# A filter regrouped inside SBUF, masks in spare rows, and a new order, in a two-part sequence layer

## The chip, the cores and the metric

One core of a Trainium2 chip. The metric is the device time of one execution in microseconds (us), median of several runs.

## The reference, cut to what matters

Two independent layers over 2048 tokens and 640 channels, their outputs side by side.

```
# A: a causal long convolution over tokens, per channel
k_shift = sum over t of k_pad[:, t:t+S] * shift_k[:, 3-t]      # short filter, 4 taps
kv = k_shift * v
y  = irfft(rfft(kv, 2S) * rfft(ssm_k, 2S))[:S] + kv * ssm_D    # long filter ssm_k: (640, 2048)
a  = q * y
# B: attention with a memory, 32 heads of 20, four segments of 512 tokens
for s in range(4):
    p     = softmax(q_s k_s^T * scale + causal mask)           # 512 x 512 per head, inside the segment
    a_dot = p @ v_s
    a_mem = phi(q_s) M / (phi(q_s) z + 1e-6)
    o     = g * a_mem + (1 - g) * a_dot
    M, z  = M + phi(k_s)^T v_s, z + sum phi(k_s)
b = concat(o) @ wo
out = concat([a, b], axis=-1)
```

## The kernel before

**Recorded, then issued by hand.** The kernel's functions do not issue instructions. They record steps (`Recorder.add`), each with an engine and a key such as `("A", 1, "FK", 0)`; `Recorder.issue` then issues all steps in the order of a list packed into the text `ORDER`, and puts each group of PSUM banks where the list `BASE` says. So every instruction of the trace carries the line of that one helper, L256, and groups are told apart by tiles. The list fixes, for each engine, the order of its instructions; SP issues nearly all DMAs, in its order.

**Part A, `conv(dp)`,** runs over five blocks of 128 channels, dp = 0 to 4. Steps of a block, by key:
- `sk`, `kt` or `sz`, `st` (`load_filter`): the long filter of the block, tokens on partitions, in tile kT, partition p holding tokens 8p to 8p+7 of either half of the sequence. Block 0 is turned by PE (`kt`). Blocks 1 to 4 go another way: a transposing DMA brings tokens 128m + p to partition p, one DMA (`sz`) writes that to a scratch in memory, the tile `turned`, and two DMAs (`st`) read it back in the wanted grouping. The ring kT has two buffers: one for the transposed load, one for the result.
- `lk`, `lc`, `lv`, `ks` (`short_filter`): k comes in transposed (kr), for blocks 2 to 4 with shifted copies (kb, kr); the 4 taps are matmuls with scaled unit matrices (skd), which ACT makes from the taps; the product with v lies in vt.
- `FK`, `FX` (`spectrum`): matmuls with the table Wf, copied out of PSUM into F by ACT or DVE as a fixed text of bits (`EVICT`) says; `BK`, `BX` are the sums behind them on DVE. `P1`, `P2`, `P3`, `YB` (`product`) are DVE work, `I` and `O` (`inverse`) matmuls with Wi, the product with q (`lq`), and the stores.

**Part B** runs over u = 0 to 7: segment u // 2, half of the heads u % 2. `project(u)`: `P` and `V` are the projections (five matmuls each); the results go to KQ, which holds per head 32 columns: 20 of k or q, one for the softmax bound, 11 zeros. `KT` is a transposing DMA from KQ to KQT, so that a head lies on 32 partitions, four heads on 128. `kam` and `bound` compute the bound, `rows` are four small DMAs that write it into row 20 of q in KQT. `attend(u)`: the steps `S` fill PSUM with scores, four heads side by side on row groups of 32: D are the four diagonal 128 x 128 blocks, A and J those below; ACT's exponential turns each into ET (160 instructions). `O` are the matmuls with Va, `N` the division, `W` the output projection, `OB` its stores.

The mask of a diagonal block is added in PSUM by matmuls ahead of the scores: four strips of 32 columns, for each head one matmul of mleft (128 columns) with mright broadcast over the four blocks.

```python
for i in range(4):
    for hl, bank, r, g in heads:
        nc.tensor.matmul(bank...[:, :, 32 * i:32 * i + 32], lhsT=self.mleft[r, 96 - 32 * i:224 - 32 * i],
                         rhs=self.mright[r, None, :].to_broadcast([32, 4, 32]), start=(i == 0), stop=False, ...)
```

Of the kernel before, what the change touches and what calls it, by code (L numbers as in the profile page):

```python
# [44 lines left out]
def small_consts():  # L45
    p = np.arange(128)
    d = p % 32
    hl = p // 32
# [4 lines left out]
    epsrow = np.zeros((128, 4), np.float32)
    for hh in range(4):
        rows = (hl == hh) & (d < DH)
        maskbd[rows, hh, 0:DH + 1] = 1.0
# [9 lines left out]
    return sel.astype(BF16_NP), maskbd.astype(BF16_NP), epsrow, mleft.astype(BF16_NP), mright.astype(BF16_NP)  # L66
# [198 lines left out]
class Layer:  # L265
    def __init__(self, ctx, tc, A_q, A_k, A_v, A_shift_k, A_ssm_k, A_ssm_D, B_x, B_wq, B_wk, B_wv, B_wo, B_beta, out):
# [18 lines left out]
        sel_np, maskbd_np, eps_np, ml_np, mr_np = small_consts()  # L285
# [36 lines left out]
        parts = [sel_np, ml_np, mr_np, np.concatenate([np.eye(64)] * 2).astype(BF16_NP), maskbd_np, eps_np.view(BF16_NP)]  # L322
# [5 lines left out]
        sel, ml, mr, id2, mb, eps = [pack[:, int(a):int(b)] for a, b in zip(at, at[1:])]  # L328
# [110 lines left out]
    def conv(self, dp):  # L439
# [8 lines left out]
        def load_filter():  # L448
            key("sk")
            sk = self.ring("kT", [128, 4, 4, 128], n=2)[:].rearrange("p a b d -> p (a b d)")  # L450
            kT = self.ring("kT", None)
            if dp in TURN:
                nc.sync.dma_start(out=sk, in_=self.ssm_k[dsl, :])
                skv = sk.rearrange("d (a p h c) -> d a h c p", a=2, h=2, c=4)
                for c in range(4):
                    key("kt", c)
                    g = self.group(1, "kt")
                    with rec.one():
                        for b in range(4):
# [65 lines left out]
        def spectrum(kind, src):  # L525
            F = self.ring("F", [128, 4, 2, 512], n=FBUF)
            for c in range(4):
                key("F" + kind, c)
                for i in range(2):
                    if i % FW == 0:  # L530
                        g = self.group(FW, "F")
                    with rec.one():
                        for j in range(2):
                            o = g.ap[:, i % FW, 256 * j:256 * j + 256]
                            last = kind == "K" and c == 0 and i == 0
                            for h in range(2):
                                rhs = src[:, h:4:2, c, :]
# [210 lines left out]
    def attend(self, u):  # L748
# [10 lines left out]
        def block(bank, hl, g, kc, q0, n, **kw):  # L759
            r = slice(32 * hl, 32 * hl + 32)  # L760
# [149 lines left out]
    def project_out(self, s):  # L910
# [41 lines left out]
        for t in range(4):  # L952
# [37 lines left out]
ORDER = r"""  # L990
c-jTQ17H{c3<SVW@|kUSwr$&9XWO=I+qOCz?QGk&&ATkfifqV^9LR}W$c;RR3P&UWrBE4VQ2}|857kf_RZs>Ikz6Z6kRRoc29Z%78Bi4kP!OR|2$c{8g^@xHd6cMwn#il^v<SLD5r|sIglLG4#E5}dh>w`as<Dwx
Q)+e8KsTh)L`aPcS{n(FUDKi-(rW`WLtXSmX0$>^?TW%$A4Rk|LL&*<ps2<}3p7Fr6hjV8hSn&iP0$@}kz0GBA&P51v_uK*jmGGKd|FbQB8#R&JM=<+O|5;<9vv_cX*G>@M1K^;P$WlZbV6JdM=4E+LRvrvql|{d
AdE(79fq7b5~&ad127gtFb2ah3S~8uPSbH1f$<oov$dQS)NPoqnYDrr*YY|=$7)J6(2UrQ%?O8FIssF)l1@Y%Ou|k~#tzKUaXJMJwIrrvu2$7XIu-MD7sl%doq=jvT_@-?jMR!6gc|x-D{C#?k186dqqL^Z#BS8l
#=2N%p^1*x+Ij%Zbua4b9xT#*SfWj}na<F9T3_d2rXIvew9rGCjiuT_Pa!GJVzQ3W`MMPywWTi5R(cL|p%zIxso64JsHYKvdFZM0aR#&__@%wIwJtyamTNC{JB|}*qbqbFW@$J5t<kK9F2YJ(itx4t6Lpn#*P~dB
wz>?HG>RO<CS9#jEV{MVc6t~~5Y-~sAKk2Lw2uzZff`wY(OK7Oc=Xl3dL3Q0i-xtExQ~81NC)e3oJW7XgcZ1esB#gPv0iT@oL#{XeTa>E73(yfZP3`Z8aEJ4hUzUmMjU&DHF$!R2xEKn0m4aiiEOJ7L*m*~tj8Vf
)n|xr`*ok*#X-G?1hxTd5mRDWB0Hel^f@}%Is};54n3>ewWGa29El}yWg}kVoNhv53)1ttRpUu)Nn)?CMf+JN+o}Dnv$eMHvRmUz1RT*_n$%t+x&2dEB6)+vlFSZi8+(VNdP<M!TLj2yO<`yBum)=q3DM))My}}z
eUFrOQa_-lwX_IwU2o`Rjc73}m0iOpw6fH4MI+fqT-D@qK|dp=rI3{J73q=CB1(7rf?jq}Q`;pCWohK5-qmkNW4H94hPK<9O43?pyRW^ihy6fSODcEtf&RmHJk%_fOnxD)^sxkzPO@1-d8FCxFMeWxrL#OX(0(I_
QPNvp>tY$Ko8_}Va7iy+Eu&?!p*GCgS_Ww$?JU1RhS(s>BzdKP6*Q5-*4Oe$A<HParLd`7vLa@Z(?Ure8E%<ngypg<QdHVWPAMz}CAa05kygywN@y8nDNx*sNf9YwxnzuWkdju^3dvZjX$7Q|WtZ<3XzeYll(v~R
&T3gTYcI3xrR9+E_Q8Hw4HH(kS611I%LEG}A5Hnwx=0l(Arq~KRJBqv$vVnp`(<UVla!RM(oK5G6dP@2th1D}3Rd1;+Y{|BrDdv>k+AZ{{#hmKBh##(RJ6VV&bD$g*ZRvRt8I1cv(>dZHr-}eDAu#r8k#MozCF_h
w$K{cb8T#8rJ=piCf3vzSu=Z~i_O`PVc6W}SvZE}5Sec+?5%#Ym%6~->0di4?YZ3ETX?o$BYv^+(t#1V!iGvq4v>|$#8z20S#1?$jXl+Y^3@`-lB~7gw#=5Aah<i2KUPs9aJ!MmC6LW{Ox9avsn5vVX*+DMHD^_6  # L1000
z$ok`QMupt*)WODjW$B6$tK%in{A|=kRXf3+T3DQq_=FfT{c{*%O3lxHRP=gk{EoiyX~DFwwSCf!PZ(rtS!H5U1`T7_Ct@_E3GBRY_J@+nml0Nv=$FqO^L;LJY;d$ij8@~x^s%mkU*&;+iaAaw9|IR&RQFuv(YkE
;_`!bVQY?&_-w+d(vjn2lGI^rcI9}PCm(gDbmC-5!1LCWb$QAb$b9L>CX$HL<g8q<gq$v?Bq@7vp`4eK(o}jfIWO8z?abahCv&8pB;zcZE3>5!FGv6zNn$491Ubz5l7fpQCHt}-8%RGkmc!Ce`tvPQ@f}lhAk*;$
(=a_>asbmZ1DD8R8N`gt!}lD_i?UQQF)#CRnLJ}=HkajcNt#I^e&BsRXJJ0%1LkKDKH>@~z#GiUUR)_dn2p()gSS|amn~R|G7EF^CWrI1tdiR-&RiVEGctn3Sb{_Og{4`BWjT_$xmwEczFd{^tiV#dD{JH_OY)OG
kZV$rW4Tt!_(b{2&w5YpSS40w6;|aqe&%?N;t_enb@GkXc*X8oS-)kkIEJJ7gZFq@Ub8xH%LbXi8m#5F?TTENpDgT?IFsw;i%w*q&tehZD6<(Nb2ynd<c@5Yn=+L}{TJtQ9&gDsPT?k*!H@jSivEe4Wjc3AG5^Es
wu+VfhCP(kEahvsO&-Zs`Od$b&jnn_MO@6%{*PN^E#X13j_X;&mvAY?E4%x0uHa5t$;WbsHT|uqKamZ5CQs!qzsoMUXH|S7H*vSTlV=vzpUYKyA@pV3BhT%nY~>FL=hrN}o9~rZQr}<8P20wOvYGY#jRbK!ckrWZ
VFTaE_fpb7$SyYWpYmBgNhtp+zhu8O_Ahck9y5%8liw1-cQdp<v?jiXb^QtdNJM{Rk$f-raX%w_RDWVo`~VN~sa5x;p3<B7KRLwIUcvuLIgjS4yoKMl=pNHwSS*k2aa<G{!yj0APv*(JxgV0ap2AytJa6S`JecYH
pj7n)p3oDyX&Vpl_@34i`)R5^wrZZ<&+sIVFo|dMOrF6{F@#5%#oKvS&*s@Zhf~k8hiCSr-r9S)>oMl^T;A4u`enBF;|#5N`~<Hsly>yIp3fV4ZtvioJiizBa}1*eyt8-l^9-k5J*-|}3Ge0wy|#zfI^Nr(X?MTK
e%{~v_$3bTfj-Im`c+2IK|a|F`CuR8Q+&0L^N2dshxu?H;n%pv$9q&A;$uCEuJkxM!K3R)ALXljhDX-KI?-qQb;i|MKF8<!XrJeiG>K02`99MZ_*!4*F*K%5^JE%NW9f8X=!-moF7_q9)R*~kkFD!{g>UdZ9$%B{
5kKk)b+2#qM7qfXbi42HoxaO=`#wMB`~A3|@PmHH4|}j5@DShZLB7Se`ZoU$7|Gh+
"""  # L1010
# [76 lines left out]
```

## Time and profile before

| | |
|---|---|
| median of 3 runs | 270.21 us (270.09 to 271.11) |
| profiled execution | 269.69 us, of which the span of the instructions 267.9 us |
| granted TensorE clock | 1.00 |
| PE, DVE, ACT busy | 258.5, 246.6, 249.2 us |
| DMA packets | 131516, 44.72 MB, of these 121899 under 512 bytes |
| memory read, written | 14.05 MB, 7.34 MB |

PE is TensorE's matmuls, PEld its weight loads, DVE VectorE, ACT ScalarE, POOL GpSimd, SP SyncE; SPq is SP's queue, which issues DMAs. A row of a timeline gives start and length in us, engine, operation, out<-in by the program's names, and a count; idle time before it stands in brackets with what ended it. A row of a group gives the count, then busy us and the mean ns of one, then idle time before it. A row of one tile's instructions gives shortest, median and longest duration in ns, then first and last start. A row of stretches gives the stretch, its length, busy us (and count) of PE, PEld, DVE, ACT and POOL, then the granted clock, the DMA engines' share, and GB/s. A row of waits: who waited for whom, us in total, how often, the longest.

### The profile page before, as it was taken

The numbers are of one execution on the slowest core, as the hardware profiler recorded it, in microseconds if no ns is written. First come the engines' busy times: TensorE is split into PE (matmuls) and PEld (weight loads), VectorE is DVE, ScalarE is ACT, GpSimd is POOL, SyncE is SP. The second block draws the span as 40 slices with busy tenths as digits, with TensorE's granted clock in tenths as the row PEclk, the third lists the DMA queues.
The fourth block names the chain that finished last, engine by engine and source line by source line (L and its number), as shares of the span: only waits on it lengthen the run. The fifth ranks groups of instructions, "written<-read, shape, count | busy, mean of one in ns | idle before, by whom it ended". The sixth has DMA issues, their size and how long they took to land.

```text
span 267.9 us, 10042 instructions
## 1 busy us (share of the span) xinstructions
PE 258.5 (96%) x4335; PEld 193.4 (72%) x4335; DVE 246.6 (92%) x387; ACT 249.2 (93%) x392; POOL 7.2 (3%) x18
## 2 busy tenths in 40 slices
PE   8999999999999999999999999999999999989994
PEld 3788678768777787878677777778776876666781
DVE  0399999999999999999999999999999999999971
ACT  2695899999999999999999999999999999999953
POOL 8200000000000000000000000000000000000000
PEclk9999999999999999999999999999999999999999
DMA  7999899988979979997997799998970194545124
GB/s 212 279 224 162 208 231 214 202 257 173 190 156 250 209 145 182 223 187 154 181 209 168 176 184 182 182 171 135 171 168 8 47 160 107 126 102 125 39 51 128
DMA packets 131516, 44.72 MB, mean 167 GB/s; under 512 B 121899, under 2 KB 129072, under 8 KB 131344
## 3 DMA queue, kind: packets, MB, share of 16 engines
q1 hardware_dynamic: 131328, 43.96, 81.3%
q8 instruction: 34, 0.56, 0.9%
q0 software_dynamic: 144, 0.12, 0.1%
q14 instruction: 10, 0.08, 0.1%
HBM read 14.05 MB, written 7.34 MB: 80 GB/s over the span
## 4 chain that ended last, share of the span: by engine, by line
PE 60%; ACT 27%; SPq 5%; issue 3%; DVE 3%; DMA 2%; ACTq 0%; DVEq 0%
PE ps L256 60%; ACT ET L256 18%; SPq L256 5%; ACT F L256 3%; DMA vt<-in_A_v_dram 2%; ACT KQ L256 2%; ACT PP L256 1%; DVE Kh L256 1%; ACT Va L256 1%; DVE vt L256 1%; ACT outb L256 1%; ACT qabs L256 0%; DVE F L256 0%; DVE kam L256 0%; ACT xT L256 0%
## 5 line engine op out<-in xcount | busy, mean ns | idle before, releaser
L256 ACT ACTIVATE ET<-ps 128x1024 bf16<-128x1024 f32 x160 | 160.4, 1092 | 0.2 <-PE ps L256 0.2
L256 PE MATMUL ps<-wqkv,xT 128*128 128x320 bf16 x480 | 77.6, 299 | 0.5 <-ACT xT L256 0.3
L256 PEld LDWEIGHTS <-xT 128*128 128x128 bf16 x640 | 57.1, 98 | 27.8 <-issue 6.8
L256 ACT CAST F<-ps 128x512 bf16<-128x512 f32 x72 | 42.4, 651 | 0.3 <-PE ps L256 0.3
L256 PE MATMUL ps<-Va,ET 128*128 128x21 bf16 x1280 | 42.0, 173 | 0.0
L256 PEld LDWEIGHTS <-ET 128*128 128x128 bf16 x1280 | 39.2, 96 | 2.3 <-issue 1.2
L256 PE MATMUL ps<-KQT 32*128 32x128 bf16 (+2 forms) x896 | 35.3, 239 | 1.0 <-DVE o L256 0.5
L256 PEld LDWEIGHTS <-Wf 128*128 128x128 bf16 x320 | 29.8, 98 | 6.3 <-issue 1.2
L256 ACT CAST KQ<-ps 128x320 bf16<-128x320 f32 x54 | 24.6, 497 | 3.3 <-PE ps L256 3.3
L256 PE MATMUL ps<-wo,xT 128*128 128x320 bf16 (+2 forms) x160 | 25.5, 299 | 1.3 <-ACT ET L256 1.3
L256 PEld LDWEIGHTS <-KQT 32*128 32x128 bf16 x896 | 16.7, 92 | 10.8 <-issue 9.3
L256 PE MATMUL ps<-kT,Wf 128*128 128x256 bf16 x160 | 22.0, 273 | 0.2 <-ACT ET L256 0.2
L256 PE MATMUL ps<-vt,Wf 128*128 128x256 bf16 x160 | 21.6, 272 | 0.0
L256 PE MATMUL ps<-Y,Wi 128*128 128x256 bf16 x160 | 20.8, 273 | 0.0
L256 DVE TENSOR_TENSOR o<-ps,rr 128x640 bf16<-128x640 f32 x24 | 19.6, 818 | 0.4
L256 DVE TENSOR_TENSOR Y<-Y,pq 128x2048 bf16<-128x2048 bf16 (+1 forms) x20 | 18.5, 936 | 0.0
L256 PE MATMUL ps<-Mbd,PqT 128*128 128x84 bf16 x96 | 18.3, 202 | 0.1
L256 DVE TENSOR_TENSOR pq<-Xh,Kh 128x2048 bf16<-128x2048 bf16 x15 | 18.2, 1212 | 0.0
L256 PEld LDWEIGHTS <-Wi 128*128 128x128 bf16 x160 | 14.8, 98 | 2.5 <-issue 0.6
L256 PE MATMUL ps<-skd,kr 128*128 128x128 bf16 (+4 forms) x116 | 16.6, 257 | 0.0
L256 PEld LDWEIGHTS <-kr 128*128 128x128 bf16 x116 | 14.6, 149 | 2.3 <-issue 1.1
L256 PE MATMUL ps<-pack 32*128 32x128 bf16 x512 | 14.8, 217 | 0.9 <-ACT ET L256 0.8
(86 smaller groups left out, 359.8 us busy)
## 6 DMA issues: line engine op xcount, KB each, us to landing
vt<-in_A_v_dram SPq DMA_DIRECT2D x10, 256.0 KB
pq<-in_A_q_dram SPq DMA_DIRECT2D x10, 256.0 KB
turned<-kT SPq DMA_DIRECT2D x4, 512.0 KB
kT<-turned SPq DMA_DIRECT2D x8, 256.0 KB
out_dram<-pq SPq DMA_DIRECT2D x8, 256.0 KB
out_dram<-outb SPq DMA_DIRECT2D x12, 160.0 KB
kb<-kr SPq DMA_DIRECT2D x6, 256.0 KB
Wf<-c_wf SPq DMA_DIRECT2D x4, 256.0 KB
```

The costliest lines, as they stand in the source:

```text
L256: f(*[fix(a) for a in args], **{k: fix(v) for k, v in kw.items()})
```

## The change

1. `load_filter`, blocks 1 to 4: the scratch in memory goes, with its write and its two reads. The transposed load is issued in two halves of 1024 tokens, interleaved in the buffer. Eight DMAs from SBUF to SBUF (`ss`, m = 0 to 7) then regroup it: each reads 128 partitions of 512 bytes and writes 16 partitions. kT's layout becomes (h, c, a, d), so that the filter's spectrum reads 256 elements in one run; block 0 copies out of PSUM into that layout.
2. The 11 spare columns of KQ are no longer zero. For the 11 token positions 116 to 126 of every 128, spare column r of k is 1 where the position is above 116 + r, and spare column r of q is -1e30 where the position equals it. So the scores matmul of a diagonal block masks those 11 query columns itself, and the fourth mask strip covers 20 columns instead of 32. Position 127 needs no mask. Score matmuls below the diagonal use 21 of the 32 rows.
3. In the set-up on POOL, the fill of 1536 elements of KQ is replaced by a small fill and two copies from the constants in `pack`.
4. ORDER and BASE are new: 1508 steps instead of 1482 (24 more on SP, 2 more on POOL). EVICT is the same text with zeros behind it that no copy reaches.

What the unpacked lists say of the order: on PE, the step `taps` moves from place 21 to place 10, straight behind the ten warm-up matmuls; the second projection P.0.3 from place 39 to 36, ahead of three of the four ks steps; three V.0 steps to places 41 to 43, ahead of all FX.0 steps; seven projections stand between the bound of u = 0 and the first S step in place of six. On ACT, four of the skd steps stand ahead of its third copy of xT in place of none. From place 60 to 490 of PE's 510 the lists differ by moves of at most six places, and at the end the W.3 steps are swapped. On SP, the eight ss of block 1 stand in the places 38 to 46, the last just ahead of the first q load of block 0.

```diff
+    spare = 31 - DH
+    own = np.arange(127 - spare, 127)
+    step = np.zeros((128, 2, spare), np.float32)
+    step[:, 0] = np.arange(128)[:, None] > own[None, :]
+    step[:, 1] = MASKED * (np.arange(128)[:, None] == own[None, :])
...
-        self.turned = [dram.tile([S, 128], bf16, name=f"turned{i}") for i in range(5)]
...
-        nc.gpsimd.memset(self.KQ[:, :, :, :, DH:32], 0.0)
+        nc.gpsimd.memset(self.KQ[:, :, 1, :, DH:DH + 1], 0.0)
         nc.gpsimd.memset(self.KQ[:, :, 0, :, DH:DH + 1], 1.0)
+        steps = step.rearrange("p (i r) -> p i r", i=2)
+        for i in range(2):
+            nc.gpsimd.tensor_copy(out=self.KQ[:, :, i, :, DH + 1:32], in_=steps[:, None, i, None, :].to_broadcast([128, 4, 16, 31 - DH]))
...
-            kT = self.ring("kT", None)
+            kT = self.ring("kT", None)[:].rearrange("p (h x) c d -> p (h x c d)", h=2).rearrange("p (h c a d) -> p h c a d", h=2, c=4, a=2)
...
-            z = self.turned[dp]
-            nc.sync.dma_start_transpose(out=sk.rearrange("p (m d) -> p m d", d=128), in_=self.ssm_k[dsl, :])
-            key("sz")
-            self.queue("sz", dp).dma_start(out=z[:].rearrange("(m p) d -> p m d", p=128), in_=sk.rearrange("p (m d) -> p m d", d=128))
-            key("st")
-            self.halves(self.queue("st", dp), kT, z, slice(0, 128))
+            sk = sk.rearrange("p (m a d) -> p m a d", m=8, a=2)
+            for a in range(2):
+                nc.sync.dma_start_transpose(out=sk[:, :, a, :], in_=self.ssm_k[dsl, 1024 * a:1024 * a + 1024])
+            for m in range(8):
+                key("ss", m)
+                nc.sync.dma_start(out=kT[16 * m:16 * m + 16].rearrange("p h c a d -> p (h c) (a d)"), in_=sk[:, m].rearrange("p a d -> p (a d)"))
             return kT
...
-                                rhs = src[:, h:4:2, c, :]
+                                rhs = src[:, h, c] if kind == "K" else src[:, h:4:2, c, :]
...
-        def block(bank, hl, g, kc, q0, n, **kw):
-            r = slice(32 * hl, 32 * hl + 32)
+        def block(bank, hl, g, kc, q0, n, rows=DH + 1, **kw):
+            r = slice(32 * hl, 32 * hl + rows)
...
                 for i in range(4):
+                    n = 32 if i < 3 else DH
                     for hl, bank, r, g in heads:
-                        nc.tensor.matmul(bank.rearrange("p (b q) -> p b q", b=4)[:, :, 32 * i:32 * i + 32], lhsT=self.mleft[r, 96 - 32 * i:224 - 32 * i],
-                                         rhs=self.mright[r, None, :].to_broadcast([32, 4, 32]), start=(i == 0), stop=False, grp=g, skip_group_check=True)
+                        nc.tensor.matmul(bank.rearrange("p (b q) -> p b q", b=4)[:, :, 32 * i:32 * i + n], lhsT=self.mleft[r, 96 - 32 * i:224 - 32 * i],
+                                         rhs=self.mright[r, None, 0:n].to_broadcast([32, 4, n]), start=(i == 0), stop=False, grp=g, skip_group_check=True)
...
-                        block(bank[:, 128 * kc:128 * kc + 128], hl, gg, kc, 128 * kc, 128, start=False, stop=(kc == 3), grp=g)
+                        block(bank[:, 128 * kc:128 * kc + 128], hl, gg, kc, 128 * kc, 128, 32, start=False, stop=(kc == 3), grp=g)
```

More of the change, by code (lines that the diff above doesn't have):

```diff
@@ L65, in small_consts @@
         mright[32 * h:32 * h + 32] = MASKED * (np.arange(32)[None, :] <= j[:, None])
-    return sel.astype(BF16_NP), maskbd.astype(BF16_NP), epsrow, mleft.astype(BF16_NP), mright.astype(BF16_NP)
+    spare = 31 - DH
[3 more added lines that the diff above has]
+    step[:, 1] = MASKED * (np.arange(128)[:, None] == own[None, :])
+    return sel.astype(BF16_NP), maskbd.astype(BF16_NP), epsrow, mleft.astype(BF16_NP), mright.astype(BF16_NP), step.astype(BF16_NP)
 QUEUES = {"sync": "SP", "scalar": "ACT", "vector": "DVE", "tensor": "PE", "gpsimd": "POOL"}
@@ L275, in __init__ @@
         rec = self.rec = Recorder(tc, psum.tile([128, 8, 512], f32, name="ps"))
-        dram = E(tc.tile_pool(name="dram", bufs=1, space=bass.MemoryType.DRAM))
-        self.turned = [dram.tile([S, 128], bf16, name=f"turned{i}") for i in range(5)]
-        rec.scratch = {t[:].tensor.name for t in self.turned}
         nc = self.nc = rec.nc
@@ L327, in __init__ @@
         nc.gpsimd.dma_start(out=pack[:], in_=self.real.inline_tensor(np.ascontiguousarray(np.concatenate(parts, axis=1)), name="c_pack").ap())
-        sel, ml, mr, id2, mb, eps = [pack[:, int(a):int(b)] for a, b in zip(at, at[1:])]
+        sel, ml, mr, id2, mb, eps, step = [pack[:, int(a):int(b)] for a, b in zip(at, at[1:])]
         self.sel, self.mleft, self.mright = sel, ml, mr
@@ L994 @@
[L994 to L997, printed above, removed]
@@ new lines @@
+t+o^smAX<(>Pr@hDM_T1RJ01#L<(CoDP?h_m86z#Qd}BIQ%Nh7tWwE(NN8ywb*#CxkjBzlN?ToPBSoy9)wg!iRsy7<w3n2UP8wKuNiQv>p(U06Qo~Y7BkL;}q^ER{;+9YbNMkD@{iL_lw8~b-I!OZQC4Ho*6|<_=
+Q98?D87>2*i6xh=(nU(jP#Gd)WxR}#(NfN8TNoK6!(^O{l&03q#z-w|Zeb;!OpsBs#n#zYn<xt`(DuoCTW&3_tSz(^w!x~{M%!j_WxJJ@7S_u$%YF$bljML*mR2@JrpjNNCNrd+wYJ_iQw~ZWn=V`BkgT*tHcNI{
+d+T7UY_WB;HrCmWN?S`NYps)Yu_ZQJw#Z@WW__)nEw!$8Oa|H<36>z+V<FPrcH0rzYyEA2ZL%KL(>B|2xhR8do`jbZGFL{~VB2Sx<f`nj(Kf`c$$UwGWwu+!*iPGT39&;K$Tqnwr)9D&lq-@53G|G_#8ew<i)5!9
+uqhUR^KwCk*+E+@6D&O@*%H|!hitj*k`!2Nhi$t|w3Ik2du5d@mEpER)>sCdlam%~X))49SVBE1>5xccAvR9gG@E6oBo0DstR1oGwo;N|nLL+cHqK_-eR(M3ZHCRU*D}|x%S^i^H{_<=mgKl2^X#P@x4V*9v*Upr
@@ new lines @@
+wJcaGCv3hwl2;O-Z)CM3#T9!jFJzs(m5q`WYb1%LK{n*TCb??w<hnhPoJgwIESWx)oAylBOJ?N84LfJ=WfV3@9>m85dv51#G(Jd5O|Gdlx_*=w79@Fb+FsgbiKb^QwWiQ~7@(izjLpCpT(p@Oi=nt|X*7b|vr9Hm
+^W(D=L|nu}di^39wE%9}Fnp8y_QY=6SIMAHtq`8s9m}K-?5;hu5BA8uOJO{=A2Jz(@zFlnTT6wED1v+PO9tr><kWYT8b9T|Wz|=f3E4EeW|Ul*h$(n&Z!9r#>1X?HU+jk^!EgC1f8?v>&~H{2KW!=|;h(4$MR{b_
+Unct7${~wFLu+oGhP0YTD<GZzv5GLAg%YTSVu+`+5lX3*5J5|#I>w<CYQQz3=GE~ijWU>z;)tUQ5L4soaKzAjIs&mYzJ}2`sEODbR_CG?@@pV!qYg@I87-*=G@RB&Ax$CSwX9Y~BrT;2QBW6QI;!9eDr<4AsO7aP
+CSWn@W3WcnC1`*uT1gwCu$It97>RnQpq)@o8>6T$Lo{~5JT$>_Y(^37jP?iuIYd{Wn65;4MrTLFX9q-J8&uU*aK>N)j?fy~7OOE-$7nmO!CF+;YC2M5GO9MiFde01bsd&sxHd;iv_L41)(KiuYw3D~W?Z($ByEL>
@@ L1014 @@
-nHs%U(_2ZGW*c8QqoCg%fTo`psW$*rt2v)JeE^7a20H
+c-mc40Tx3c2r@Fg|BYuzt?l<}S&B$*n3>x$)HKVQqik5vo@MQOD;u>R^obhId#g1Wjq**}qh^%V-$vUO>UY*y^xS7zW6E-2Y%FK4WRAv#axO*$eIR=fcL-^afeXjDJLnzf_r6(<T8-@TVFWVWo_)U=*`tJuWk?^0
+Q4l%E%2k0AHCZQ=%cy2&4&gSoUAyy7zCu!05Yxyn=ws4i(hi*;l>Q(*Fmg(1NRuG1t`=0FU$)uAMfmRVSBJ6I)^9O>P=}BOt<D^aUD7P$YI^j8lz^%`=dKDj>#1IdAGKU8@$iLS4N|7>mO4JwJ%?%Bk?Pv@VEWSs
+_{(#0xL)72H+4a%+fK|;(DnLIy>UCj)d5Gl{x7<H0JDz<QU
 """
```

37 lines of the change are left out of this document (15 added, 22 removed).

## The prediction

> **What bounds the kernel now.** I read the page first, then busy time by stretch of the run, then single rows where the change touches them. The page:
>
> ```profile
> span 267.9 us, 10042 instructions
> PE 258.5 (96%) x4335; PEld 193.4 (72%) x4335; DVE 246.6 (92%) x387; ACT 249.2 (93%) x392; POOL 7.2 (3%) x18
> DVE  0399999999999999999999999999999999999971
> ACT  2695899999999999999999999999999999999953
> DMA  7999899988979979997997799998970194545124
> PE 60%; ACT 27%; SPq 5%; issue 3%; DVE 3%; DMA 2%; ACTq 0%; DVEq 0%
> ```
>
> No engine is the bound alone: PE, ACT and DVE are all above 92%, and the chain changes hands. The slices say where the holes are: the first three or four (some 25 us) and the last two. The windows split the run at ACT's first copy out of PSUM (6.2 us) and near its first exponential; columns are length, then busy time of PE, PEld, DVE, ACT and POOL:
>
> ```profile
> 0.00:6.20 6.20, 4.91 (x15) 1.86 (x15) 0.33 (x1) 1.28 (x1) 4.95 (x15) 1.00 0.70 197
> 6.20:33.60 27.40, 26.82 (x264) 21.11 (x265) 21.88 (x39) 21.08 (x55) 2.24 (x5) 1.00 1.00 222
> 33.60:256.00 222.40, 218.40 (x3955) 164.80 (x3955) 219.88 (x340) 222.13 (x330) 0.00 (x0) 1.00 0.83 163
> 256.00:268.00 12.00, 8.41 (x105) 5.62 (x102) 4.50 (x9) 4.68 (x8) 0.00 (x0) 1.00 0.38 100
> ```
>
> From 33.6 to 256 us ACT is idle for 0.27 us, DVE for 2.5, PE for 4.0. So in four fifths of the run nothing can be won unless work leaves ACT, and none does: every exponential and every copy out of PSUM stays, on the same engine. What is left: ACT's 6.3 idle us between 6.2 and 33.6, and the tail. In the head PE itself is idle for only 0.58 of 27.4 us, and DMA is at 1.00: the head is bound by PE and loads, not by ACT.
>
> **The change part by part.**
>
> Masks. Eleven of 32 columns of each diagonal block are masked by the spare rows of the scores matmul, so the fourth mask strip has 80 columns instead of 128.
>
> ```profile
> L256 PE MATMUL ps<-pack 32*128 32x128 bf16 x512 | 14.8, 217 | 0.9 <-ACT ET L256 0.8
> 131.17 0.40 PE L256 MATMUL ps<-pack 32*128 32x128 bf16 x16
> 131.40 0.39 PE L256 MATMUL ps<-KQT 32*128 32x128 bf16 x16
> ```
>
> 512 mask matmuls are 32 fills of 16, in quads that run side by side on four row groups: 16 take 0.23 us from start to start (131.17 to 131.40), a quad 58 ns. 48 of 128 columns off one quad is 22 ns, times 32 fills 0.69 us of PE. Bounds: nothing (ACT covers it: 0.27 us idle) and -0.69. I take -0.4, since PE holds 60% of the chain. The other score fills now use 21 of each 32 rows; columns and row groups are the same, so I cost that at nothing (a rival below).
>
> Filter, on the DMA engines. Per block the change removes a 512 KB write to the scratch and two reads of 256 KB, and adds 512 KB from SBUF to SBUF in 512-byte pieces; the transposed load is split into two halves of the same bytes.
>
> ```profile
> 33.00:60.00 27.00, 26.52 (x431) 19.74 (x431) 26.61 (x38) 26.98 (x45) 0.00 (x0) 1.00 1.06 227
> 141.00:144.00 3.00, 3.00 (x36) 2.10 (x35) 3.00 (x6) 3.00 (x5) 0.00 (x0) 1.00 1.09 219
> ```
>
> Where DMA is full (share 1.06) it moves 227 GB/s, so 1 MB less is an estimated 4.6 us of a full queue. The nearest row for SBUF to SBUF is the second: there the 64-partition copies kb<-kr run, at 219 GB/s, so the new 512 KB cost about 2.4 us. Net -2.2 us of DMA per block, -9 in all. On the path it is worth nothing: in the page's chain DMA holds 2%, all of it one early load of vt. Bounds 0 and -0.3.
> The Trainium skill, SBUF — State Buffer, section Door 1: The DMA port swizzle, speaks against the transfers: partitions 0 to 15 reach 4 of 16 ports and were measured at 104 GB/s, 0 to 63 reach 8 at 196 GB/s. The trace is near it for 64 (219 GB/s); by the page the eight transfers, 16 destination partitions each, would take an estimated 5 us a block, and the relief would be gone.
>
> Filter, on SP's queue.
>
> ```profile
> L256 SPq DMA_DIRECT2D kb<-kr x6: 550/586/595, 53.2 to 140.9; - x6
> L256 SPq DMA_DIRECT2D kT<-turned x8: 438/534/606, 46.1 to 192.1; - x8
> L256 SPq DMA_TRANSPOSE kT<-in_A_ssm_k_dram x4: 2030/2306/2758, 31.8 to 165.0; - x4
> L256 SPq DMA_DIRECT2D turned<-kT x4: 454/568/757, 37.1 to 177.3; - x4
> SPq L256 <- PE ps L256: 39.9, 16, 4.1
> SPq L256 <- DVE outb L256: 14.4, 5, 3.7
> ```
>
> Eight issues at 0.59 (the row of kb<-kr) are 4.7 us; the three removed were 0.57 + 2 x 0.53 = 1.6. So SP has 3.1 us more per block, 12 in all, and the halved transposed load costs its 2.3 again (up to +0.5). SP waits far longer than that (54 us for these two releasers alone), so in blocks 2 to 4 it is covered. The first of the eight waits for both transposes to land, where before the write waited for one and the read for the write; behind it in the queue stand the next block's transposed k, the q loads and the rows transfers. Tight is block 1:
>
> ```profile
> 52.56 0.58 SPq L256 DMA_DIRECT2D kT<-turned  x1
> 53.24 1.18 SPq L256 DMA_DIRECT2D kb<-kr  x2
> 54.47 0.80 SPq L256 DMA_DIRECT2D Wi<-c_wi  x1
> 55.37 1.47 SPq L256 DMA_DIRECT2D pq<-in_A_q_dram  x1
> 60.78 0.27 PE L256 MATMUL ps<-kT,Wf 128*128 128x256 bf16 x1
> ```
>
> The last of the eight stands just ahead of that first q load. 55.4 + 3.1, less the two kb copies now behind it (1.2), puts it near 57; the filter's first matmul needs it at 60.8. I take 0 on the path; ends 0 and +3. That matmul and its rate do not change: rows with one run of 256 and with two runs of 128 elements cost the same.
>
> ```profile
> L256 PE MATMUL ps<-kT,Wf 128*128 128x256 bf16 x160 | 22.0, 273 | 0.2 <-ACT ET L256 0.2
> L256 PE MATMUL ps<-Y,Wi 128*128 128x256 bf16 x160 | 20.8, 273 | 0.0
> ```
>
> POOL. A fill of 1536 elements gives way to one of 64 and two copies of 704.
>
> ```profile
> 2.91 1.40 POOL L256 MEMSET KQ<- 128x1536 bf16 x1
> 6.01 0.40 POOL L256 MEMSET KQ<- 128x64 bf16 x1
> 8.06 0.38 POOL L256 MEMSET PP<- 128x64 bf16 x1
> 17.89 2.04 SPq L256 DMA_TRANSPOSE KQT<-KQ  x1
> ```
>
> No POOL copy is in the trace: by the fill's 0.91 ns an element 0.64 us each, at four times that 2.6. POOL then ends at 8.44 - 1.0 + 1.3 to 5.2 = 8.7 to 12.6 us; the first reader, a transpose of KQ, goes out at 17.9. Nothing on the path at either end; if that cover were gone the copies would cost their own 1.3 to 5.2.
>
> Order. I unpacked both lists and set them side by side. From PE's 60th step to its last W steps nothing moves by more than six places; the head is really rearranged. The taps matmuls and their copy go first instead of at 11 us; P.0.3 goes ahead of three ks steps; three V steps go ahead of the FX steps.
>
> ```profile
> 11.01 0.63 PE L256 MATMUL ps<-ident,qabs 5*64 5x5 bf16 x12
> 11.98 0.35 ACT L256 ACTIVATE skd<-pack,taps 128x64 bf16<-128x64 bf16 x1 [1.20 <-DVE taps L256]
> 21.69 0.84 PE L256 MATMUL ps<-wqkv,xT 128*128 128x320 bf16 x5
> 22.57 0.43 ACT L256 CAST KQ<-ps 128x320 bf16<-128x320 f32 x1 [2.47 <-PE ps L256]
> 32.96 0.40 PE L256 MATMUL ps<-pack 32*128 32x128 bf16 x16
> 33.64 1.96 ACT L256 ACTIVATE ET<-ps 128x1024 bf16<-128x1024 f32 x2
> ```
>
> The skd scalings depend on the taps alone, so with early taps they fill ACT's gaps (the 1.20 goes). The gap of 2.47 before the cast of P.0.3 goes too; late next is the cast of V.0.0, now third of the V steps behind ks, so much of that gap returns two places on. What counts is the work that ACT has behind it when the exponentials start. By the lists that is one skd (0.35) and one KQ cast (0.43) more, each a row's duration: 0.8, or about 0.6 without the part that overlaps its neighbour. Against it the first S step stands behind one more projection: five matmuls, from 21.69 to the next step at 22.37, 0.68. PE has at most 0.58 idle to give back up to there and 0.3 before 6.2. So ACT's gain is 0.6 - 0.68 + (0 to 0.9): -0.1 to +0.8, and I take 0.4. Bounds for the order as a whole: -3 (half of ACT's 6.3 idle us) and +1.
>
> Tail. The last W steps are swapped; same count, same last chain: matmul, ACT's copy, store. Nothing.
>
> Sum: masks -0.4, filter 0, POOL 0, order -0.4, tail 0: -0.8 us. The profiled execution took 269.69 (span 267.9 and 1.8 around it), so it would become 268.9; it lies 0.5 below the median of 270.21, and against that median the sum is 269.4.
>
> **The rivals.** 0.5% (1.35 us) is about what can be told from no change, so faster begins below 268.86 and slower above 271.56.
>
> A, the head wins more. If early taps let half of ACT's 6.3 idle us before the exponentials close, and DVE, idle 5.5 us in the same window, follows: -2.3 to -3, around 267.2. For it: DVE has 2.5 us of slack later. Against: PE has 0.9 idle us in the whole head, and PE feeds ACT there.
>
> B, slower: the filter of block 1 arrives late. In a full queue the eight transfers land one behind the other. If they go at half the row's 219 GB/s, 512 KB take 4.8 us, and begun near 52 to 53 behind the backlog of a queue at 1.06 the last lands after 60.8. From there each late us is a us of PE, as the matmul stands in PE's order with everything behind it, and ACT has 0.27 us to absorb it. Three us late: 269.4 + 3 = 272.4. Half the rate is what 4 ports in place of 8 amount to in the Trainium skill, SBUF — State Buffer, section Door 1. Against: 3 us of margin, and less DMA traffic ahead of it.
>
> C, nothing moves: PE's 0.69 us is covered by ACT, the relief of DMA touches no wait, the head only trades gaps. 270.2.
>
> D, the head loses: the V steps ahead of FX hold back the spectrum of X, on which DVE's longest run hangs; up to two V steps at 0.68: +1.4, 271.6.
>
> E, matmuls of 21 rows no longer run four side by side: a fill of 4 x 512 columns would take four times a quad's 0.23 us, +0.7 on 48 fills, about 303. The trace has no row tile with fewer than 32 rows in use.
>
> **How the numbers follow.** My forecast (between -0.3 and -1.6) 0.40, C 0.15, A 0.23, B 0.13, D 0.07, E 0.02. Faster is A and the lower fringe of the forecast (0.05): 0.28. Same is the rest of the forecast and C: 0.50. Slower is B, D and E: 0.22. The likeliest case's own range is 268.6 to 269.9. The range to give reaches into A and into B: 267.2 to 271.8, with some 5% left out below and 12% above.
>
> **What would show it.** Masks: rows of ps<-pack with 32x80 moving operands, 128 of them. Filter: no tile named turned, 32 issues kT<-kT of about 0.59 us, about 8 points less DMA share in the middle, and no idle time of PE ahead of ps<-kT,Wf at 59 to 61 us. Head: first skd near 6.5 us instead of 11.98, first ET between 33.0 and 34.0, ACT's idle time between 6.2 and 33.6 down from 6.3 to about 5.5. Wrong it would be through a PE wait on a kT transfer, a first ET later than 34.5 or earlier than 32, or ACT idle in the middle.

## The result: 0.7% slower, with the loss in block 3

Changed kernel 272.3 us (median of 7), kernel before 270.09 in the same comparison: ratio 1.0069, 95% interval 1.0044 to 1.0095. The forecast was 269.4, its range 267.2 to 271.8. The profiled execution took 272.3, its span 270.4. Ratios, here and below, leave out executions that fell in a slower state of the chip, medians do not, so a median can lie up to 1.6 us above what its ratio gives. From the page of the changed kernel:

```profile
span 270.4 us, 10078 instructions
PE 258.2 (95%) x4335; PEld 192.4 (71%) x4335; DVE 246.4 (91%) x387; ACT 249.6 (92%) x392; POOL 7.3 (3%) x20
DVE  1669799999999999999999969999999999999971
ACT  2894999999999999999999979999999999999953
q1 hardware_dynamic: 126656, 41.86, 82.2%
```

Every engine's busy time is what it was; the span is 2.5 us longer, so the loss is waiting. The slice rows say where: in mid-run one digit of DVE is 6 and one of ACT 7 (the 24th slice, 155 to 162 us), where all were 9. The windows of the changed kernel, split as before (length, then busy time of PE, PEld, DVE, ACT, POOL; clock; DMA share; GB/s):

```profile
6.20:33.60 27.40, 26.55 (x229) 20.26 (x226) 21.01 (x38) 21.33 (x56) 2.13 (x4) 1.00 0.99 215
33.60:256.00 222.40, 215.99 (x3922) 162.38 (x3921) 218.41 (x338) 220.05 (x327) 0.00 (x0) 1.00 0.85 154
140.00:160.00 20.00, 19.54 (x341) 14.71 (x334) 19.18 (x30) 19.41 (x34) 0.00 (x0) 1.00 0.83 167
160.00:180.00 20.00, 18.59 (x306) 13.62 (x304) 18.01 (x30) 18.71 (x28) 0.00 (x0) 1.00 1.16 177
```

ACT, idle for 0.27 us from 33.6 to 256 before, is idle for 2.35 now, 1.88 of it between 140 and 180. Its same instruction lies 0.73 us later than before at the first exponential (34.37 for 33.64), 0.1 to 0.3 later at 70 to 98, 0.4 at 153, and 2.2 to 2.7 later from 162 on. So the head's loss was won back, and what stays arises within some 15 us, in block 3. The timeline there (start, duration, engine, instruction, and in brackets idle time and what ended it):

```profile
157.20 1.05 PE L261 MATMUL ps<-kT,Wf 128*128 128x256 bf16 x8 [0.46 <-DMA kT<-kT]
161.82 0.40 PE L261 MATMUL ps<-KQT 21*128 21x384 bf16 x8 [1.23 <-DMA KQT<-qabs]
161.96 0.49 DVE L261 TENSOR_SCALAR qabs<-KQ 128x1280 bf16<-128x1280 bf16 x1 [2.58 <-DMA KQT<-qabs]
162.27 1.02 ACT L261 ACTIVATE ET<-ps 128x1024 bf16<-128x1024 f32 x1 [1.05 <-PE ps L261]
```

Two transfers are late: the filter of block 3 (kT<-kT) and, behind it, the four small rows transfers of unit 4 (KQT<-qabs, 4 KB each). Both wait for their turn to be issued, on SP:

```profile
142.14 1.30 SPq L261 DMA_DIRECT2D kT<-kT  x2
143.48 1.23 SPq L261 DMA_DIRECT2D kb<-kr  x2
144.75 0.60 SPq L261 DMA_DIRECT2D kT<-kT  x1
145.46 3.49 SPq L261 DMA_TRANSPOSE PqT<-PP  x1
149.05 0.61 SPq L261 DMA_DIRECT2D pq<-in_A_q_dram  x1
149.72 1.94 SPq L261 DMA_DIRECT2D kT<-kT  x3
151.70 0.61 SPq L261 DMA_DIRECT2D pq<-in_A_q_dram  x1
152.35 1.96 SPq L261 DMA_DIRECT2D kT<-kT  x2
154.36 0.59 SPq L261 DMA_DIRECT2D out_dram<-outb  x1
155.00 0.51 SPq L261 DMA_DIRECT2D kr<-kr  x1
155.60 1.23 SPq L261 DMA_DIRECT2D KQT<-qabs  x2
```

Read the starts against the durations: each issue begins where the one ahead ends. The two further rows went out at 157.58. In the kernel before, from its timeline of SP, the first two rows went out at 148.78, and SP has gaps: 3.26 us ahead of the kr<-kr copy and 1.72 us ahead of a KQT transpose.

```profile
140.30 1.19 SPq L256 DMA_DIRECT2D kb<-kr  x2
144.75 0.46 SPq L256 DMA_DIRECT2D kr<-kr  x1
148.78 1.18 SPq L256 DMA_DIRECT2D KQT<-qabs  x2
150.00 0.61 SPq L256 DMA_DIRECT2D pq<-in_A_q_dram  x1
152.33 1.28 SPq L256 DMA_TRANSPOSE KQT<-KQ  x1
```

Counted from such rows between 131 and 157 us, gaps of more than 0.15 us add up to 5.3 us before and to nothing after. The view of waits gives more for the same 26 us, 10.0 and 3.4 in all, and its largest rows (total, times, longest) show why it is not idle time; first before, then after:

```profile
SPq L256 <- PE ps L256: 5.2, 2, 2.7
```
```profile
SPq L261 <- PE ps L261: 3.0, 1, 3.0
```

The 3.0 us belong to the PqT transpose, which is shown from 145.46 to 148.95 right behind the issue ahead of it: the view lets a wait end inside the row of the issue itself. So the gaps between rows are the number to go by. The eight issues took 5.8 of SP there (1.30, 0.60, 1.94 and 1.96) and the transposed load of block 3, issued at 98 before, stands at 131.85 now (2.7); the two old reads (1.05) are gone. That is 7.4 us more for 5.3 us of gaps.

### The profile page after: what moved, and what is told of

It is laid out like the page before. It is cut to its first block, busy times and chain, and to the rows that moved or that the text cites. A ratio compares the mean times of both kernels' runs of the same rounds, so it can differ in the third digit from the quotient of the medians.

```text
span 270.4 us, 10078 instructions
## 1 busy us (share of the span) xinstructions
PE 258.2 (95%) x4335; PEld 192.4 (71%) x4335; DVE 246.4 (91%) x387; ACT 249.6 (92%) x392; POOL 7.3 (3%) x20
## 3 DMA queue, kind: packets, MB, share of 16 engines
q1 hardware_dynamic: 126656, 41.86, 82.2%
## 4 chain that ended last, share of the span: by engine, by line
PE 61%; ACT 19%; DVE 10%; DMA 4%; issue 3%; SPq 2%; POOL 0%; DVEq 0%; ACTq 0%; POOLq 0%
PE ps L261 61%; ACT ET L261 12%; ACT F L261 2%; SPq L261 2%; DVE vt L261 2%; DMA kT<-kT 2%; DVE Kh L261 1%; DMA vt<-in_A_v_dram 1%; DMA qabs<-in_A_shift_k_dram 1%; ACT Va L261 1%; ACT PP L261 1%; DVE F L261 1%; DVE o L261 1%; DVE PP L261 1%; DVE Y L261 1%
## 5 line engine op out<-in xcount | busy, mean ns | idle before, releaser
L261 ACT CAST F<-ps 128x512 bf16<-128x512 f32 x72 | 43.4, 659 | 0.9 <-PE ps L261 0.9
L261 PE MATMUL ps<-KQT 32*128 32x128 bf16 (+3 forms) x896 | 35.9, 239 | 1.6 <-DMA KQT<-qabs 1.2
L261 ACT CAST KQ<-ps 128x320 bf16<-128x320 f32 x54 | 25.6, 510 | 0.4 <-PE ps L261 0.3
L261 PEld LDWEIGHTS <-KQT 32*128 32x128 bf16 (+1 forms) x896 | 16.2, 92 | 11.6 <-issue 9.7
L261 ACT CAST Va<-ps 128x320 bf16<-128x320 f32 x31 | 15.1, 505 | 4.0 <-PE ps L261 4.0
```

The costliest lines, as they stand in the source:

```text
L261: f(*[fix(a) for a in args], **{k: fix(v) for k, v in kw.items()})
```

## The experiments

Theory: SP's in-order queue is full in block 3, and what stands behind the eight issues is late (called Queue, later Number, where its time counts, and Rows or Places, where the order within it counts). Rivals: Contention (bytes and ports on the DMA engines), Order or Compute (the new order of PE, DVE and ACT), Masks. Each run was timed in five rounds beside the kernel before; the ratio is to it.

**One part at a time.** Masks alone, in the kernel before:

```diff
-        nc.gpsimd.memset(self.KQ[:, :, :, :, DH:32], 0.0)
+        nc.gpsimd.memset(self.KQ[:, :, 1, :, DH:DH + 1], 0.0)
+            nc.gpsimd.tensor_copy(out=self.KQ[:, :, i, :, DH + 1:32], in_=steps[:, None, i, None, :]...
-            r = slice(32 * hl, 32 * hl + 32)
+            r = slice(32 * hl, 32 * hl + rows)
+                    n = 32 if i < 3 else DH
```

> The kernel before, its order and its scratch, with only the masks changed (128 strips of 80 columns for 128, score fills of 21 rows, POOL's two copies). Masks as forecast: 269.5 (0.4 less); covered by ACT: 270.0; if the masks cost something in the changed kernel: above 270.5.

270.24, ratio 1.0001 (0.9985 to 1.0016). The masks are worth nothing that shows; the interval reaches from -0.4 to +0.4 us. Filter alone, in the kernel before:

```diff
-transposed load | write to the scratch | read | read
+two half loads  | kT<-kT x3            | x3   | x2       (same places of SP's queue)
```

> The kernel before, its order and its masks, with nothing changed but the filter: two halves of the transposed load at the place of the load, and three, three and two of the eight transfers at the places of the write and the two reads. Queue: in this order the load of block 3 goes out at 98 and the transfers between 124 and 148, and SP waits 10 us between 131 and 157, so it is covered: 269.8 to 270.6. Contention: about 272 as in the changed kernel. Order or Masks: 270.1, no cost from the transfers at all.

270.63, ratio 1.0023 (1.0003 to 1.0043): about a third of the loss, and hardly clear of none. All but the filter, in the changed kernel, and then the scratch in block 3 alone:

```diff
-two half loads, kT<-kT x8
+if dp in VIA:   # (1, 2, 3, 4), then (3,)
+    one transposed load; write at the place of the first kT<-kT; reads at those of the fifth and sixth
```

> The changed kernel with its masks and its order, but all four blocks through the scratch in memory (one transposed load, one write, two reads at the places of the second half and of the first, fifth and sixth of the eight transfers). Queue: as with block 3 alone, 269.6 to 270.4, since the other blocks never waited. Contention: 269.6 to 270.4 as well, but clearly below the run with block 3 alone. Order: 272.3; Masks: 272.3.

> The changed kernel, but block 3 alone regroups its filter through the scratch in memory again: one transposed load at the place of the second half, the write at the place of the first of the eight transfers, the two reads at the places of the fifth and sixth. Blocks 1, 2 and 4 keep the eight transfers. Queue: SP gets 3 us back between 131 and 154, rows of unit 4 go out near 151 to 154, time 270.0 to 270.6. Contention: a quarter of the loss goes with one of four blocks, about 271.7. Order or Masks: 272.3.

With all four blocks 272.42 (1.0085, 1.0063 to 1.0108), with block 3 alone 271.08 (1.0031, 1.0008 to 1.0054; its runs spread from 269.47 to 272.8). The first seems to speak against the theory: the transfers are gone from all blocks, SP has six issues less in each, and the loss is there. But SP's time in block 3 did not become less. In its timeline the issues behind the write to the scratch are longer, PqT 5.12 us for 3.49 in the changed kernel; from 131 to 157 SP again has no gap of more than 0.15 us, and the rows go out 0.7 us later still:

```profile
141.21 0.53 SPq L261 DMA_DIRECT2D turned<-kT  x1
144.54 5.12 SPq L261 DMA_TRANSPOSE PqT<-PP  x1
156.28 1.27 SPq L261 DMA_DIRECT2D KQT<-qabs  x2
```

So this run has fewer issues in a queue that is as full, and does not part the queue's time from the order within it. Its profile has DVE waiting 1.7 us for KQT<-qabs in block 3 again, and new losses at 73 us (0.35) and near 107 (0.8), whose cause its waits do not name.

**The rows.** The four rows transfers of unit 4 put ahead of what they stood behind, with the eight transfers and with block 3 through the scratch:

```diff
-... kT<-kT | out_dram<-outb | kr<-kr | KQT<-qabs x2 | vt | KQT<-qabs x2
+... kT<-kT | KQT<-qabs x4 | out_dram<-outb | kr<-kr | vt
```

> The changed kernel with one thing moved: the four rows transfers of unit 4 (KQT<-qabs, 4 KB each) go right behind the eighth kT<-kT transfer of block 3 in SP's queue, ahead of one store (out_dram<-outb), the kr<-kr copy and the load of vt that they stood behind: out at about 154.4 to 156.8 in place of 155.6 to 158.7. Eight transfers, masks and the order of PE, DVE and ACT stay. Theory Rows (the loss at 162 is the rows transfers standing too far back in SP's queue, whatever regroups the filter): the waits at 161.8 and 162.0 shrink by 1.2 to 2, the wait of 0.5 to 0.8 for kT<-kT at 157.2 stays, time 270.3 to 271.2. Theory Contention (DMA full, the rows land late wherever they are issued): 272 to 272.6. Theory Order of PE, DVE and ACT, or Masks: 272.3.

> The run with block 3 alone through the scratch, and the four rows transfers of unit 4 right behind the second load of q, ahead of the store and the kr<-kr copy. Rows: the run with the scratch alone still had 1.2 us of PE and 1.8 of DVE waiting for these rows; they go, time 269.3 to 270.0, at or below the kernel before. Contention: 271. Order or Masks: 271.

271.56 (1.0047, 1.0029 to 1.0064) and 270.24 (0.9998, 0.9979 to 1.0016). The medians put the rows alone at 0.7 to 0.8 in both pairs (272.3 to 271.56, 271.08 to 270.24); the intervals overlap, so neither pair is clear of the noise by itself. With the eight transfers the rest only moved on, to the next in the queue:

```profile
169.91 0.85 PE L261 MATMUL ps<-wqkv,xT 128*128 128x320 bf16 x5 [1.17 <-DMA xT<-in_B_x_dram]
```

With the scratch in block 3 and the rows ahead the whole loss is gone (clear of the noise against the changed kernel), and no engine waits for a transfer behind the head. This version moves more bytes than the changed kernel (1.5 MB in block 3 for 1). Its queue, with six issues less in block 3 and the rows out at 152.34:

```profile
149.77 1.33 SPq L261 DMA_DIRECT2D kT<-turned  x2
152.34 2.67 SPq L261 DMA_DIRECT2D KQT<-qabs  x4
```

**SP's time by itself.** To the last version six issues of 512 bytes each, which nothing reads, at places of the missing transfers of block 3:

```diff
+nc.sync.dma_start(out=self.idle[:, 0, m], in_=self.ident[0:16, 0:16])   # m = 0..5
```

> The run with block 3 through the scratch and the rows of unit 4 moved ahead (270.24, no wait on a transfer of block 3), plus six SP issues of 16 partitions x 32 bytes that nothing reads, at the places where the changed kernel has six more of its transfers in block 3: some 3.5 us of SP and no bytes. Number (SP's time in block 3 is what the eight transfers cost there): the loss comes back, 271.2 to 272.3, with waits between 155 and 175. Contention (the bytes of the eight transfers on the DMA engines cost it): 270.2, nothing comes back.

274.09 (1.0132, 1.0097 to 1.0167): 3.9 us lost for six issues that move next to nothing; the three executions at a granted clock of 1.00 took 272.79 to 273.52, the three at 0.994 took 274.65 to 274.8. The rows go out at 156.74 in place of 152.34, and late by turns are a buffer of outb, the x load and (1.33 us, at 174.43) KQT:

```profile
161.16 0.42 ACT L261 CAST outb<-ps 128x320 bf16<-128x320 f32 x1 [1.64 <-DMA out_dram<-outb]
171.76 0.85 PE L261 MATMUL ps<-wqkv,xT 128*128 128x320 bf16 x5 [0.65 <-DMA xT<-in_B_x_dram]
```

So SP's time by itself, without the bytes, is enough for the loss of block 3; that the bytes cost nothing beside it is not shown. The same issues in the kernel before, eight a block and three a block:

> The kernel before with nothing but SP issues added: in each of the blocks 1 to 4 eight transfers of 16 partitions x 32 bytes that nothing reads, three, three and two behind the old write and the two old reads, some 4.8 us of SP a block and no bytes worth counting. Number (SP's time is what the eight transfers cost in the old order, where they cost 0.7): 270.6 to 271.5. Contention (their bytes cost): 270.1.

> The kernel before with three of the empty SP issues in each of blocks 1 to 4, one behind the old write and one behind each old read: 1.8 us of SP a block where eight cost 14.2 us in all. If SP's time is on the path throughout, three eighths of it: 275.4. If SP's queue has a slack of 3 us or so in each block, beyond which every us counts: 270.1 to 270.8.

Eight: 284.28 (1.0495, 1.0451 to 1.054), 13.4 us by the ratio. Three: 269.66 (0.9978, 0.996 to 0.9995), nothing lost. So the old order takes 1.8 us more a block and does not take 4.7 (eight issues of 0.587 median). My 270.6 to 271.5 for eight was far too low: I still thought of the slack as large. The gaps do not make it so, because a gap is not free for every issue: the 3.26 us ahead of kr<-kr are a wait for the kb<-kr copies to land, and with the eight issues ahead of it that gap is still there, 4.3 us (150.98 to 155.28).

Not all of the 13.4 is SP's time. In the profiled execution of the eight (284.81) the granted clock is 0.50 in three stretches, the longest from the end of a PE gap of 3.47 us on:

```profile
161.20:168.00 6.80, 6.14 (x40) 4.00 (x40) 6.16 (x9) 5.47 (x8) 0.00 (x0) 0.50 0.66 139
```

The other two last 3.4 us each, from 72.5 and 243.1. At half the clock the 13.6 us hold up to 6.8 us less of PE's work, an estimate from these stretches. The kernel before shows the price of one. A mean clock of 0.994 is what one stretch of 3.4 us gives, as in the profiled execution of the filter alone; of the 17 executions of the kernel before beside the run with three issues, six at 0.994 took 271.01 to 271.47, the others (0.998 to 1.00) 269.45 to 270.26, so about 1.1 us. None of the twelve with three issues is at 0.994, and that alone can put their ratio below 1. How much of the loss is SP's alone stays open.

**Order against places.** SP's queue of the one kernel, behind block 1, with the compute order of the other:

```diff
-SP: order of its own kernel
+SP: own order up to block 1's last kT<-kT, then that of the other kernel (PE, DVE, ACT unchanged)
```

> The changed kernel (its masks, its eight transfers, its order of PE, DVE and ACT, and its SP queue up to the eighth transfer of block 1), but from there on SP issues in the order of the kernel before, with three, three and two of the eight transfers at the places of the old write and the two old reads. Theory Places (what costs is where the new order of SP's queue puts the transposed load of block 3, the rows of unit 4, the x load, PqT): as the old order with the eight transfers, 270.2 to 271.0, no wait for KQT<-qabs at 162. Theory Compute (the new order of PE, DVE and ACT costs): 272.3. Theory Number (eight issues for three, wherever they stand): between, 271 to 272.

> The reverse: the order of PE, DVE and ACT and the masks of the kernel before, its SP queue up to the eighth transfer of block 1, and from there on SP's order of the changed kernel, with the eight transfers. Places: 272 to 273, with waits for kT<-kT and KQT<-qabs between 155 and 172. Compute: 270.6, as the old order with the eight transfers. Number: 270.6 to 271.5.

> As the first of these, but through the scratch in all four blocks: the masks, the order of PE, DVE and ACT and the head of the changed kernel, with the old filter at the old places of SP's queue. Places: 269.6 to 270.3; what is left of the difference to the kernel before is the new head and the masks alone (forecast 0.8 less). Compute: 272.4, as the run with the scratch in the new places.

272.4 (1.0076), 274.78 (1.0172) and 271.97 (1.0066). Places as I put it is refuted by the first and third: with the old queue the new order takes as long as with its own (272.4 for 272.3). But the first loses elsewhere. Behind block 3 ACT lies no later against the kernel before than ahead of it (1.9 us at 166, 2.0 at 149), where it lost 2.1 us in the changed kernel; the time goes between 77 and 89 us and near 119, in small waits, most on other transfers (vt<-in_A_v_dram 0.7, KQT<-KQ 0.3 and 0.5). Its profiled execution, at 273.62 the longest of six, also has a stretch at half the clock, from 252.7. In the second the stall of block 3 went along with the queue into the old compute order (the first filter matmul of block 3):

```profile
158.66 1.05 PE L256 MATMUL ps<-kT,Wf 128*128 128x256 bf16 x8 [1.68 <-DMA kT<-kT]
```

So the old compute order loses about 4 us under the changed queue (274.78 for the 270.63 of its own queue with the same transfers), the new one nothing under the old queue. Why the new compute order loses some 2 us under the old queue, and with the scratch in all blocks under either (272.42 and 271.97), is not shown.

**Three ways to relieve SP, all misses.** The load and the transfers of block 3 moved earlier; the 32 transfers on POOL's queue; the mid-run stores on POOL's queue, in the changed kernel and in the kernel before:

```diff
-A.3 half loads at 131.9, kT<-kT x8 at 142 to 153
+A.3 half loads behind kr<-kr (109.5), kT<-kT x8 behind rows of unit 3 (127)
-nc.sync.dma_start(out=kT[16 * m:16 * m + 16]...
+nc.gpsimd.dma_start(out=kT[16 * m:16 * m + 16]...
-STQ = 1
+STQ = 0    # out_dram<-pq and out_dram<-outb of the middle from POOL
```

> The changed kernel with one thing moved: in block 3 the two halves of the transposed filter load go right behind the kr<-kr copy of block 3 (about 109.5 us in place of 131.9) and the eight kT<-kT transfers behind the fourth rows transfer of unit 3 (about 127.5 in place of 142 to 153). All engines but SP keep their order. Theory Queue (SP's in-order queue in block 3 is full, the last kT<-kT lands after PE wants it and the four rows transfers go out behind it): the waits of PE at 157.2 (0.5 to 0.8 us) and of PE and DVE at 161.8 to 162.0 (1.2 and 2.6) go, SP has idle time again between 131 and 157, time 270.0 to 270.5. Theory Contention (eight transfers of 16 partitions each take DMA time wherever they are issued): 272 to 272.6, the waits move to other transfers. Theory Order (the new order of PE, DVE and ACT costs the 2 us) or Masks: unchanged at 272.3.

> The changed kernel with the 32 kT<-kT transfers issued from POOL's queue in place of SP's; same transfers, same bytes, same order of everything else. Queue: SP loses 5 us of issues in each block, the rows transfers of unit 4 go out 4 to 5 us earlier, no wait at 157 or 162: 269.6 to 270.3. Contention: the transfers take the same DMA time and PE still waits: 272. A rival of its own: POOL's transfers are slower to issue or to land, and PE waits ahead of ps<-kT,Wf in several blocks: above 273.

> The changed kernel with the stores of A's blocks 0 to 3 and of B's first three rows of tiles issued from POOL's queue in place of SP's: 20 issues of 0.5 to 2 us off SP, the eight transfers as they are. Number: SP runs ahead, no wait at 157 or 162: 270.0 to 270.8. Contention or Compute: 272.3. A rival: POOL's stores land late and what reuses their buffers waits: above 272.5.

> The kernel before with the same stores on POOL. SP gets 10 to 20 us back, but ACT is idle for 0.27 us only between 33.6 and 256, so there is nothing to win: 269.8 to 270.3. If the stores land late from POOL: above 271.

276.76 (1.0227), 281.96 (1.0381), 276.72 (1.0212), 275.31 (1.0155). The first shows Queue from its other side: the two loads now stand ahead of KQT transposes of unit 3 and the eight transfers ahead of those of unit 4, and with these the buffer KQ comes free late, which ACT and PE need:

```profile
139.95 0.43 ACT L261 CAST KQ<-ps 128x320 bf16<-128x320 f32 x1 [3.89 <-DMA KQT<-KQ]
140.43 0.84 PE L261 MATMUL ps<-wqkv,xT 128*128 128x320 bf16 x5 [3.10 <-ACT KQ L261]
141.50:148.30 6.80, 6.63 (x76) 3.67 (x76) 6.36 (x11) 4.89 (x9) 0.00 (x0) 0.50 1.14 208
```

The last line is a window of the same kernel: after that gap PE's granted clock is 0.50 from 141.5 to 148.3; ACT's same instruction lies 5.7 us later than in the kernel before at 140 us, and 8.4 at 151, so the last 2 us or so fall in that stretch. From POOL the transfers land 7.1 us after their issue in the median (for SP's queue the trace has no landing times), and block 1, whose margin I had called tight, has none (tile view and timeline of the run with the transfers on POOL):

```profile
L261 POOL DMA_DIRECT2D kT<-kT x32: 528/528/587, 47.5 to 183.6; - x32
DMA to landing us min/median/max: 4.0/7.1/13.2
64.48 1.01 PE L261 MATMUL ps<-kT,Wf 128*128 128x256 bf16 x4 [2.64 <-DMA kT<-kT]
```

Nor did SP, rid of these transfers, get time in block 3: its rows fill 24.6 of the 26 us from 131 to 157 in that run, as they fill 24.5 in the changed kernel. The stores on POOL land late, as the rival named beforehand had it. In the old order the profiled execution (273.68, the shortest of six) has ACT at most 0.7 us late up to 238 and 3.9 from 247 on; between them ACT waits for a buffer of outb, PE stands still for 1.13 and 0.72 us, and the granted clock is 0.50:

```profile
240.48 0.42 ACT L256 CAST outb<-ps 128x320 bf16<-128x320 f32 x1 [1.73 <-DMA out_dram<-outb]
241.90:245.30 3.40, 3.40 (x55) 2.39 (x55) 1.68 (x3) 2.79 (x3) 0.00 (x0) 0.50 0.02 5
```

What the longer executions lost beyond that is not on record. No version here beats the kernel before by what can be told.

## Why the prediction was wrong, step by step

- **Filter, on SP's queue**: the step that failed. The issue was sized right (0.608 us median measured, 0.59 taken), and so was the split load:

```profile
L261 SPq DMA_DIRECT2D kT<-kT x32: 585/608/1646, 48.9 to 202.7; - x32
L261 SPq DMA_TRANSPOSE kT<-in_A_ssm_k_dram x8: 1239/1318/3092, 39.5 to 171.1; - x8
```

  "In blocks 2 to 4 it is covered" was not: I set 3.1 us a block against 54 us of waits, a sum over the run from a view that counts time in which SP issues. The gaps had to be counted in the stretch ahead of the transfers that someone needs, where there were 5.3, and the load that moved from 98 to 132 into this stretch had to be counted too: 7.4 us more to issue there, not 3.1. Two signs that I had named for being wrong are there: PE waits on a kT transfer (0.46 us at 157.2), and ACT is idle in the middle (2.35 us). That the queue goes on in order, so that 4 KB rows behind the eight issues stop DVE, I had named for what stands behind but priced for block 1 only. Block 1 itself was right: no wait on a transfer ahead of its first filter matmul, now at 61.63, though the q load behind the eight went out at 59.11, not near 57. Rival B came to the measured time (272.4) by another way, transfers that are slow to land in block 1; that the number agrees is luck.
- **Filter, on the DMA engines**: 2.2 us a block of relief, taken as worth nothing on the path. The relief did not come: 82.2% of 270.4 us is 222.3 us of queue time, 81.3% of 267.9 was 217.8, with 2.1 MB less; DMA's share in the middle is 0.85 for 0.83, not 8 points less. My row was misread: 219 GB/s is all that moved in that window, not the copies' own rate. Those two of 256 KB, issued from 140.30, held up SP until 144.75, some 118 GB/s, an estimate from these two times. Here the rule that I weighed and set aside (the Trainium skill, SBUF — State Buffer, section Door 1: The DMA port swizzle) was nearer than my row: 16 partitions are not 64. No run times the eight transfers by themselves, so this is argued, not shown. Whether it is these bytes or SP's time that cost the 0.6 us in the old order stays open.
- **Masks**: -0.4 taken, bounds 0 and -0.69. The rows are there (strips of 80 columns, 128 of them), a matmul takes 194 ns for 217, and alone the masks give 1.0001, with -0.4 at the edge of its interval. That ACT covers the rest is argued from its 0.27 idle us. Rival E is out: 21-row fills take as long as 32-row ones (329 ns here for 384 columns, 330 before).

```profile
L261 PE MATMUL ps<-pack 32*128 32x80 bf16 x128 | 7.1, 194 | 0.0
L261 PE MATMUL ps<-KQT 21*128 21x384 bf16 x128 | 13.7, 329 | 1.6 <-DMA KQT<-qabs 1.2
L261 POOL COPY KQ<-pack 128x704 bf16<-128x704 bf16 x2 | 1.5, 784 | 0.0
```

- **POOL**: right; the copies take 0.784 us each, in the lower part of 0.64 to 2.6, and nothing waits.
- **Order**: -0.4 taken. The first skd went to 6.32 as forecast, but the first exponential came 0.73 later, not earlier, and ACT's idle time in the head fell by 0.25 only, to 6.07: the gap returned at the cast of V.0.0, as I had said, and at 4.03 us it is longer than the 2.47 it replaces. Behind the head this made no difference. The version with the new order and no wait in block 3 is at 0.9998 of the kernel before: the gain that I forecast is not there, and the order need not cost anything. What it did was to set SP's queue, and that I read only for the compute engines ("nothing moves by more than six places") and not for SP, where the load moved by 34 us.
- **Tail**: right, nothing.

## What to carry to other kernels

Price an issuing queue as an engine: its rows and the gaps between them in the stretch ahead of each due transfer, not waits over the run, and with every transfer that the new order moves into that stretch. Ask of each gap what it waits for: one that waits for a transfer of its own queue is not free for the issues ahead of it. Trading one large transfer for several small ones takes slots, and behind the last free slot the time comes back at whatever stands next in the order: six empty issues cost some 3 to 4 us here, and the bytes saved were no set-off. An order of issues goes with an order of compute: the old compute order lost about 4 us under the changed queue. And look at the granted clock before calling a loss the price of what was added: one stretch at 0.50 cost about 1.1 us here.

## What the runs showed of the hardware that I had not expected

- Issues behind a large write took longer. Three empty issues behind the 512 KB write to the scratch took 4.66 us (the first of them 3.4), where the median of the 32 is 0.587:

```profile
37.93 0.70 SPq L256 DMA_DIRECT2D turned<-kT  x1
38.67 4.66 SPq L256 DMA_DIRECT2D idle<-ident  x3
```

  The Trainium skill, Perfetto Trace Analysis, section DMA Instruction — HWDGE (DVE, Sync), says that an issue is shown from the end of its semaphore waits, with the wait for the descriptor generator in it; this row agrees, though no run separates the two.
- The granted clock fell to 0.50 behind PE gaps of 3.10 us (141.5 to 148.3, the run with block 3 moved earlier), and behind far shorter ones: in the profiled execution of the filter alone in the old order (272.87, the longest of twelve) no gap ahead of such a stretch is longer than 1.28 us.

```profile
77.83 0.22 PE L256 MATMUL ps<-skd,kr 128*128 128x128 bf16 x1 [1.28 <-DVE vt L256]
78.20:81.60 3.40, 3.40 (x21) 2.11 (x19) 3.40 (x8) 1.08 (x2) 0.00 (x0) 0.50 1.00 218
```

  In the changed kernel a gap of 1.23 us left it at 1.00, so the length of a gap does not settle it. The Trainium skill, TensorE: Matmul & The Clock Gate, section Part 1: The HAM clock gate (the "warmup" mystery), gives one idle window of some 3.4 us for the fall to half; the trace does not agree, as PE was never idle for that long ahead of 78.2.
- POOL's queue was idle and still no relief: moved there, transfers and stores cost some 4 to 8 us by the ratios against the kernel that they were taken from, part of it in stretches at half the clock.
